# Talking-heads attention and two expert layers: the half-empty fourth key block of the V product done in 64x64 quarters

## The chip, the cores and the metric

The kernel runs on one core of one Trainium2 chip. The metric is the time of one execution on the device in microseconds (us), given as the median of several runs. All arithmetic is in 32-bit floating point.

## What is computed

The reference chains three layers. Only the first is touched by the change.

```python
# _attn_ref: batch 4, 12 heads, 448 positions, head size 64
scores = scale * np.matmul(q, k.transpose(0, 1, 3, 2))
scores = np.einsum('bhij,hg->bgij', scores, w_pre)
scores = scores - np.max(scores, axis=-1, keepdims=True)
attn = np.exp(scores)
attn = attn / (np.sum(attn, axis=-1, keepdims=True) + 1e-09)
attn = np.einsum('bhij,hg->bgij', attn, w_post)
return np.matmul(attn, v).astype(np.float32)
# reference
x = np.ascontiguousarray(attn_out.transpose(0, 2, 1, 3)).reshape(B * S, H * D)
x = _moe_ref(x=x, **moe_kwargs)        # x @ w_in, ELU, @ w_out
return _moe2_ref(x=x, **moe2_kwargs)   # x @ w_in, h * softmax(h), layer norm, @ w_out
```

The last matrix product of the attention, attn times v, is what this text calls the V product.

## The kernel before, in words

The 448 query rows of each of the four batches are cut into chunks, 17 in all (`CH`): nine of 120 columns, two each of 110, 98 and 88, one of 80 and one of 40. The chunk is the unit of the scores (L587) and of the V product (L741).

Between these two the work goes by slots of ten query rows, taken two at a time as a unit; there are 90 units. For each unit TensorE mixes the heads (`pre`, L659, into `pm`), VectorE takes the maximum (L664), ScalarE the exponential (L669, into `e`), and GpSimd scales the post-mixing weights by the reciprocal sums (L680, into `wr`). `post` (L692) multiplies the two, which mixes the heads again and turns the result over at once, so that keys lie on partitions: 28 matmuls of 64 output partitions by 60 columns into the two banks `po`. One copy per slot (L700) moves `po` to the chunk's tile `at`.

Keys are counted in blocks of 64, and 448 keys are seven of them. In `at` two blocks lie on the 128 partitions, so there are four such pairs (q = 0 to 3), and the fourth holds one block only. The kernel before fills it so: the five rows r = 0 of a slot have the seventh block on partitions 0 to 63, the five rows r = 1 have it on 64 to 127, zeros lie in the other half (`po` is cleared once at the start), and the tile of v holds the seventh block twice. The V product of a chunk is then 2 halves n of six heads, each with 24 matmuls: three pairs i of heads, four key blocks q, two heads k. The two heads of a pair go to the output partitions 0 to 63 and 64 to 127. Each half has a bank of PSUM (`sc`), which one copy (L748) empties into a tile `x`, and a DMA stores that to the scratch tensor `xs`, from which the first expert layer reads.

Each of these steps is an `op` with a rank (a planned time), the engines that may take it with a planned cost each, and the buffers that it needs. `schedule` replays the list with these costs and writes each engine's program in the order that results; six banks of PSUM are shared between the scores, `pm` and the V product. TensorE and the other engines then work through their programs strictly in that order and wait on semaphores. `AV` is the planned cost of 24 matmuls of the V product. Towards the end of the attention the first matmuls of the expert layer (L357, output `h` or `sc`) are planned in between.

## Time and profile before

| | |
|---|---|
| median of 3 runs | 1052.45 us (1050.37 to 1053.49) |
| the profiled execution, its own time | 1048.23 us |
| its span, first to last instruction | 1046.4 us |
| TensorE busy | 1017.5 us, 97% |
| VectorE, ScalarE, GpSimd busy | 742.7, 561.8, 271.2 us |
| granted TensorE clock, mean | 0.998 |

The attention takes about the first 358 us of the span; everything after it is the two expert layers. In the trace a 32-bit matmul of the attention is two instructions, so 24 matmuls of the program stand as x48. In the chain of work each piece lasts from the end of the piece before it to its own end. A matmul that gives partitions 0 to 63 and one that gives 64 to 127 can run beside each other, as can matmuls that read different halves of the 128 rows.

### The profile page before, as it was taken

What the parts mean: (1) busy time and instruction counts of PE and PEld (TensorE: products, weight loads), DVE (VectorE), ACT (ScalarE), POOL (GpSimd) and SP (SyncE); (2) the same over time, 40 slices, a digit from 0 to 9 for tenths busy, and PEclk for the clock granted to TensorE, in tenths of its full rate; (3) what the DMA queues carried; (4) which work ended last, traced back from release to release, by engine and by line L of the source; (5) the groups of instructions that cost most, each with busy time, mean ns of one, the idle gap of its engine ahead of it and who ended that gap; (6) DMA issues with size and microseconds to landing.
All of it is one profiled execution on the core that took longest, in us unless ns stands there. A gap on an engine that the chain in (4) does not pass through costs nothing.

```text
span 1046.4 us, 28479 instructions
## 1 busy us (share of the span) xinstructions
PE 1017.5 (97%) x11604; PEld 865.4 (83%) x11604; DVE 742.7 (71%) x1365; ACT 561.8 (54%) x1186; POOL 271.2 (26%) x295
## 2 busy tenths in 40 slices
PE   6799999999999999999999999999999999999998
PEld 2476776787777999889899999999999888889998
DVE  5587777678676447898979687786855355668874
ACT  3387667677778566443444344434443245555543
POOL 5011111111113324545535434434544200000000
PEclk9999999999999999999999999999999999999999
DMA  6666766876855452534523422422472533828741
GB/s 210 210 193 200 233 200 213 237 228 209 242 165 188 138 153 84 193 126 155 177 80 122 134 98 99 138 81 71 136 296 98 201 114 106 187 106 202 150 102 60
DMA packets 142442, 165.79 MB, mean 158 GB/s; under 512 B 79496, under 2 KB 119272, under 8 KB 142312
## 3 DMA queue, kind: packets, MB, share of 16 engines
q1 hardware_dynamic: 135817, 142.62, 45.7%
q0 software_dynamic: 3968, 17.30, 4.2%
q10 hardware_dynamic: 2527, 4.06, 1.2%
q8 instruction: 91, 1.49, 0.6%
q14 instruction: 39, 0.32, 0.1%
HBM read 88.02 MB, written 37.22 MB: 120 GB/s over the span
## 4 chain that ended last, share of the span: by engine, by line
PE 84%; DVE 5%; DMA 4%; issue 2%; ACT 2%; POOL 1%; ACTq 1%; POOLq 0%; DVEq 0%; SPq 0%
PE h L357 18%; PE o L898 18%; PE h L1026 11%; PE w L1098 10%; PE sc L741 7%; PE po L692 7%; PE sc L587 6%; PE pm L659 6%; DMA sp<-sev 2%; DVE x L914 1%; DVE wy L213 1%; ACTq L545 1%; PE sc L357 1%; DMA ws<-in_wi_dram 1%; ACT e L669 1%
## 5 line engine op out<-in xcount | busy, mean ns | idle before, releaser
L898 PE MATMUL o<-gh,woh 128*128 128x448 f32 x384 | 141.3, 368 | 2.8 <-DVE x L914 2.8
L898 PE MATMUL o<-glo,woh 128*128 128x448 f32 x384 | 140.0, 364 | 0.0
L898 PE MATMUL o<-gh,wol 128*128 128x448 f32 x384 | 139.6, 364 | 0.0
L669 ACT ACTIVATE e<-pm,st 128x448 f32<-128x448 f32 x180 | 115.1, 653 | 42.0 <-DVE st L664 34.3
L692 PEld LDWEIGHTS po<-wr,e 60*64 60x64 f32 x5040 | 98.6, 134 | 34.6 <-issue 18.9
L914 DVE TENSOR_TENSOR x<-x,o 128x448 f32<-128x448 f32 x168 | 102.6, 613 | 28.9 <-PE o L898 27.7
L587 PE MATMUL sc<-kt,q 64*64 64x448 f32 x816 | 106.7, 557 | 11.8 <-ACT sev L593 5.8
L664 DVE TENSOR_REDUCE st<-pm 128x1 f32<-128x448 f32 x180 | 106.0, 617 | 15.5 <-PE pm L659 14.1
L680 POOL TENSOR_TENSOR wr<-wpost_t,st 128x120 f32<-128x120 f32 x90 | 35.7, 397 | 284.5 <-DVE st L676 170.2
L692 PE MATMUL po<-wr,e 60*64 60x60 f32 x5040 | 103.0, 220 | 5.4 <-ACT at L700 2.3
L369 POOL TENSOR_TENSOR glo<-g,gh 128x448 fp32r<-128x448 f32 x64 | 78.2, 1221 | 113.4 <-ACT gh L368 110.7
L357 PE MATMUL h<-xh,wih 128*128 128x448 f32 x276 | 100.8, 365 | 0.0
L357 PE MATMUL h<-xh,wil 128*128 128x448 f32 x276 | 100.7, 365 | 0.0
L357 PE MATMUL h<-xl,wih 128*128 128x448 f32 x276 | 100.4, 364 | 0.0
L659 PE MATMUL pm<-sp,wpre_t 64*64 64x448 f32 x720 | 96.5, 545 | 3.4 <-ACT e L669 2.4
L1026 PE MATMUL h<-wi,x2h 128*128 128x512 f32 x308 | 98.8, 395 | 0.8 <-issue 0.8
L741 PEld LDWEIGHTS sc<-at,v 128*64 128x64 f32 x1632 | 76.3, 139 | 14.2 <-ACT e L669 3.5
L741 PE MATMUL sc<-at,v 128*64 128x120 f32 (+5 forms) x1632 | 83.4, 259 | 0.6 <-ACT sev L593 0.5
L898 PEld LDWEIGHTS o<-gh,woh 128*128 128x128 f32 x384 | 72.1, 188 | 11.0 <-DVE x L914 5.7
L898 PEld LDWEIGHTS o<-glo,woh 128*128 128x128 f32 x384 | 72.0, 188 | 6.1
L898 PEld LDWEIGHTS o<-gh,wol 128*128 128x128 f32 x384 | 72.1, 188 | 5.5
L587 PEld LDWEIGHTS sc<-kt,q 64*64 64x64 f32 x816 | 41.2, 136 | 40.4 <-ACT sev L593 12.2
(130 smaller groups left out, 2014.5 us busy)
## 6 DMA issues: line engine op xcount, KB each, us to landing
sp<-sev SPq DMA_DIRECT2D x90, 210.0 KB
ws<-in_wi_dram SPq DMA_DIRECT2D x33, 512.0 KB
ws<-in_wo_dram SPq DMA_DIRECT2D x21, 512.0 KB
lts<-sq SPq DMA_DIRECT2D x14, 512.0 KB
lt<-lts SPq DMA_DIRECT2D x56, 128.0 KB
q<-in_qa_dram SPq DMA_DIRECT2D x34, 192.0 KB
v<-in_vt_dram SPq DMA_DIRECT2D x24, 256.0 KB
wis<-ws POOLq DMA_DIRECT2D x12, 512.0 KB, 3.3
```

Source lines behind the costliest of these rows:

```text
L357: nc.tensor.matmul(ps[:, :S], a[:, kc * FG + ft * 128:kc * FG + (ft + 1) * 128], x[:, kc, :], start=kc == 0 and n == 0, stop=kc == ECH - 1 ...
L369: nc.gpsimd.tensor_tensor(glo, g, f(gh), ALU.subtract)
L587: nc.tensor.matmul(T[key][i][64 * x:64 * x + 64, :S], q[sl, h % 6 // 2, 64 * x:64 * x + 64], k[sl, :], start=True, stop=True)
L659: nc.tensor.matmul(ps_t[u][r][64 * s:64 * s + 64, :S], wpre_t[p, :], sp_t[c][p, g, :], start=True, stop=True)
L664: nc.vector.tensor_reduce(out=st_t[u][:P, r:r + 1], in_=ps_t[u][r][:P, :S], op=ALU.max, axis=AX.X, negate=True)
L669: nc.scalar.activation(out=t[:P], in_=ps_t[u][r][:P, :S], func=AF.Exp, bias=st[:P, r:r + 1], scale=1.0, accum_out=st[:P, 2 + r:3 + r])
L692: nc.tensor.matmul(out[:, :, 5 * r:5 * r + 5], e_t[u, r][sl, 64 * n:64 * n + 64], wr_t[u][sl, r].rearrange("p (g a) -> p g a", a=5), start ...
L741: nc.tensor.matmul(ps[64 * k:64 * k + 64, i, :], v_t[CH[c][0]][:, 6 * n + 2 * i + k, q, :], at_t[c][:, q, 6 * n + 2 * i + k, :w], start=q ...
L898: nc.tensor.matmul(ps[:, :S], a[:, ft * DM + e * 128:ft * DM + (e + 1) * 128], x, start=n == 0, stop=n == 5)
L914: nc.vector.tensor_tensor(x1[tb][:, e, :], x1[tb][:, e, :], ps[:, :S], ALU.add)
L1026: nc.tensor.matmul(ps[:, hf * 512:hf * 512 + 512], a[:, k, :], w, start=n == 0, stop=n == 3 * ECH - 1)
L1098: nc.tensor.matmul(ps[:, :384], a[:, s, k, :], w, start=k == 0 and i == 0, stop=k == 3 and i == 2)
```

## The change

The fourth key block is taken out of the 128-row matmuls and done in matmuls of 64 rows, 64 output partitions and half the columns, which is a quarter of the array each.

- `at` has a new layout: 84 lines of five rows per slot. For q below 3 a line is one (q, head, r); for q = 3 there are only the 12 heads, with r = 0 on the lower and r = 1 on the upper partitions. `post` writes `po` so, without zeros; the copy per slot is 420 elements wide and not 480, and the two clearings of `po` go.
- `whole` is what remains of the V product of a half n: 18 matmuls, with the columns ordered r = 0 first, then r = 1.
- `halves` does the fourth block: 12 matmuls. In the first group (swap 0) the lower rows, r = 0, go to the bank of n = 0 and the upper rows, r = 1, to the bank of n = 1; in the second group (swap 1) it is crossed over. So the two halves of the rows never write to one bank at the same time.
- After swap 0 half of each bank is complete: r = 0 of n = 0 and r = 1 of n = 1. Two copies take these halves out. Swap 1 is made to wait for both, and two more copies take out the other halves. The stores come behind them.
- The planned costs change: `AV` 2.6 to 1.96, `AVQ` .35 for a group of quarters, and those of the copies.
- The width of the last chunk of a batch is now the full number of slots: 90 and 100 columns in place of 88 and 98.

```diff
--- before.py
+++ after.py
@@ -503,7 +503,7 @@
 
 
     t_pre, t_post, t_av, t_sc = {}, {}, {}, {}
-    PRE, POST, AV, SC, HID = .76, .83, 2.6, .76, 3.64
+    PRE, POST, AV, AVQ, SC, HID = .76, .83, 1.96, .35, .76, 3.64
     t, nf, t_hid = T0, 0, None
 
     def plan_front():
@@ -523,7 +523,7 @@
         if pending and u - pending[0][0] == 3:
             for k in pending.pop(0)[1]:
                 t_av[k] = t
-                t += AV
+                t += AV + AVQ
         for c in range(NC):
             if last_of[c] == u:
                 pending.append((u, [(c, 0), (c, 1)]))
@@ -616,8 +616,6 @@
     def clear(t, us, r):
         return op(r, lambda e: nc.gpsimd.memset(t, 0.0), pool=us)
 
-    for t in po_p:
-        op(T0 + 2, lambda e, t=t: nc.vector.memset(t, 0.0), dve=.49)
     o_clear = {c + 3: clear(sp_t[c][:, CH[c][2]:], .38 * (NH - CH[c][2]), 4.0 + c) for c in range(2)}
 
     def begin(e):
@@ -688,17 +686,15 @@
                 for r, n, q, x in todo:
                     for s in range(ns):
                         sl = slice(64 * s, 64 * s + 60)
-                        out = ps[s][64 * x:64 * x + 64, q * 120:q * 120 + 120].rearrange("p (g a) -> p g a", a=10)
-                        nc.tensor.matmul(out[:, :, 5 * r:5 * r + 5], e_t[u, r][sl, 64 * n:64 * n + 64],
+                        out = ps[s][64 * x:64 * x + 64, :420].rearrange("p (l a) -> p l a", a=5)
+                        nc.tensor.matmul(out[:, 24 * q + r:24 * q + 24:2] if q < 3 else out[:, 72:], e_t[u, r][sl, 64 * n:64 * n + 64],
                                          wr_t[u][sl, r].rearrange("p (g a) -> p g a", a=5), start=True, stop=True)
 
         def take(e, s, u=u, sl=sl):
             c, g = sl[s]
             if c not in at_t:
-                at_t[c] = pools["at"].tile([128, 4, NH, WMAX], F32, tag="at", name="at")
-            o, n = 10 * g, min(10, width_of(c) - 10 * g)
-            copier(e)(at_t[c].rearrange("p q h r -> p (q h) r")[:, :, o:o + n],
-                      po_t[u][s][:, :480].rearrange("p (x a) -> p x a", a=10)[:, :, :n])
+                at_t[c] = pools["at"].tile([128, 84, WMAX // 2], F32, tag="at", name="at")
+            copier(e)(at_t[c][:, :, 5 * g:5 * g + 5], po_t[u][s][:, :420].rearrange("p (l a) -> p l a", a=5))
 
         r0 = t_pre[u]
         pre_op[u] = o = op(r0, pre, [o for c in {c for c, _ in sl} for o in sp_op[c]] + [o_begin, w_op], pmb, [spb_[c] for c in {c for c, _ in sl}], pe=PRE)
@@ -713,7 +709,7 @@
         o = op(r0, post, ex + [ow], pob, eb + [wb], pe=POST)
         for s, (c, g) in enumerate(sl):
             at_ops[c].append(op(r0 + 1.2 + .1 * s, lambda e, s=s, take=take: take(e, s), [o], [at_b[c]] if g == 0 else [],
-                                [pob[s]] + ([at_b[c]] if g else []), act=.45, dve=.57))
+                                [pob[s]] + ([at_b[c]] if g else []), act=.41, dve=.52))
 
 
     for c in range(NC):
@@ -729,31 +725,55 @@
 
             for i in range(6):
                 ov.append(op(t_av[c, 0] - VD + 4 * i if b else T0 + 8 + 2.5 * i, lambda e, i=i, load=load: load(e, i), [o_begin], [] if i else [vb], [vb] if i else [], sp=.5, lag=4.0))
+        G = CH[c][2]
+        av_of, x_of = [Buf("sc", range(6 if c else 3)) for _ in range(2)], [Buf("x") for _ in range(2)]
+
+        def whole(e, n, c=c, G=G, av_of=av_of):
+            x_t[c, n] = av_of[n].tile()[:, :30 * G].rearrange("p (k w) -> p k w", k=3)
+            for i in range(3):
+                for q in range(3):
+                    for k in range(2):
+                        h = 6 * n + 2 * i + k
+                        nc.tensor.matmul(x_t[c, n][64 * k:64 * k + 64, i, :], v_t[CH[c][0]][:, h, q, :], at_t[c][:, 24 * q + 2 * h:24 * q + 2 * h + 2, :5 * G],
+                                         start=i == 0 and q == 0, stop=False, skip_group_check=True)
+
+        def halves(e, swap, c=c, G=G):
+            for i in range(3):
+                for r in range(2):
+                    n, p = (r + swap) % 2, slice(64 * r, 64 * r + 64)
+                    for k in range(2):
+                        h = 6 * n + 2 * i + k
+                        m = nc.tensor.matmul(x_t[c, n][64 * k:64 * k + 64, i, 5 * G * r:5 * G * r + 5 * G], v_t[CH[c][0]][p, h, 3, :], at_t[c][p, 72 + h, :5 * G],
+                                             start=False, stop=swap == 1, skip_group_check=True)
+                        if swap and i == 0:
+                            for x in T["half", c]:
+                                tc.add_manual_dep(m.ins, x.ins.name, mybir.DependencyInfo(mybir.DependencyClass.Sync, mybir.DependencyReason.DATA), reason="halves")
+
+        def second(e, whole=whole, halves=halves):
+            whole(e, 1)
+            halves(e, 0)
+
+        part = 10 * G / 120
+        o = op(t_av[c, 0], lambda e, whole=whole: whole(e, 0), at_ops[c] + ov, av_of[:1], [vb, at_b[c]], pe=AV * part)
+        o = op(t_av[c, 1], second, [o], av_of[1:], [vb, at_b[c]] + av_of[:1], pe=AV * part + AVQ)
+
+        def take(e, n, r, c=c, G=G):
+            if r == n:
+                T["x", c, n] = pools["xt"].tile([128, 3, WMAX], F32, tag="x", name="x")
+            T.setdefault(("half", c), []).append(copier(e)(T["x", c, n][:, :, :10 * G].rearrange("p k (g r a) -> p k g r a", r=2, a=5)[:, :, :, r],
+                                                           x_t[c, n][:, :, 5 * G * r:5 * G * r + 5 * G].rearrange("p k (g a) -> p k g a", a=5)))
+
+        def store(e, n, c=c, w=w):
+            b, r, _ = CH[c]
+            dst = xs[b][n * 384:n * 384 + 384, r:r + w]
+            dma(dst.rearrange("(k p) w -> p k w", k=3), T["x", c, n][:, :, :w])
+
+        r0 = t_av[c, 1] + AV
+        first_half = [op(r0 + .4 + .1 * n, lambda e, n=n, take=take: take(e, n, n), [o], [x_of[n]], [av_of[n]], act=.28, dve=.26) for n in range(2)]
+        o = op(r0 + .9, lambda e, halves=halves: halves(e, 1), first_half, [], [vb, at_b[c]] + av_of, pe=AVQ)
         for n in range(2):
-            r = t_av[c, n]
-            xb, avb = Buf("x"), Buf("sc", range(6 if c else 3))
-
-            def mm(e, c=c, n=n, w=w, avb=avb):
-                ps = x_t[c, n] = avb.tile()[:, :3 * w].rearrange("p (k w) -> p k w", k=3)
-                for i in range(3):
-                    for q in range(4):
-                        for k in range(2):
-                            nc.tensor.matmul(ps[64 * k:64 * k + 64, i, :], v_t[CH[c][0]][:, 6 * n + 2 * i + k, q, :], at_t[c][:, q, 6 * n + 2 * i + k, :w],
-                                             start=q == 0, stop=q == 3)
-
-            o = op(r, mm, at_ops[c] + ov, [avb], [vb, at_b[c]], pe=AV * w / 120)
-
-            def take(e, c=c, n=n, w=w):
-                T["x", c, n] = pools["xt"].tile([128, 3, WMAX], F32, tag="x", name="x")
-                copier(e)(T["x", c, n][:, :, :w], x_t[c, n])
-
-            def store(e, c=c, n=n, w=w):
-                b, r, _ = CH[c]
-                dst = xs[b][n * 384:n * 384 + 384, r:r + w]
-                dma(dst.rearrange("(k p) w -> p k w", k=3), T["x", c, n][:, :, :w])
-
-            o = op(r + AV + .2, take, [o], [xb], [avb], act=.36, dve=.42)
-            T["xs", c, n] = op(r + AV + 1, store, [o], [], [xb], sp=.5, more=.2)
+            o2 = op(r0 + .9 + .6 + .1 * n, lambda e, n=n, take=take: take(e, n, 1 - n), [o], [], [av_of[n], x_of[n]], act=.28, dve=.26)
+            T["xs", c, n] = op(r0 + .9 + 1.5, lambda e, n=n, store=store: store(e, n), [o2, first_half[n]], [], [x_of[n]], sp=.5, more=.2)
 
 
     last = None
```

On TensorE, around the second half of chunk 2 (120 columns; `sc<-kt,q` are scores, `pm` is `pre`, `po` is `post`, `sc<-at,v` the V product), the order before is:

```order
L692 MATMUL po_109<-wr,e 64x12x5
L587 MATMUL sc<-kt,q 64x448 x4
L741 MATMUL sc<-at,v 64x120 x24
L587 MATMUL sc<-kt,q 64x448 x4
L659 MATMUL pm<-sp,wpre_t 64x448 x4
L587 MATMUL sc<-kt,q 64x448 x4
L692 MATMUL po_108<-wr,e 64x12x5
```

And at the same place after the change:

```order
L690 MATMUL po_109<-wr,e 64x60
L587 MATMUL sc<-kt,q 64x448 x4
L737 MATMUL sc<-at,v 64x120 x18
L746 MATMUL sc<-at,v 64x60 x12
L587 MATMUL sc<-kt,q 64x448 x4
L657 MATMUL pm<-sp,wpre_t 64x448 x4
L746 MATMUL sc<-at,v 64x60 x12
L690 MATMUL po_108<-wr,e 64x12x5
```

The 24 matmuls have become 18 with the first group of quarters right behind them; four score and four `pre` matmuls then stand between the two groups.

On ScalarE the copies of chunk 2 stand so before (`sev<-sc` takes scores out, `e` is the exponential, `at<-po` the copy per slot):

```order
L748 COPY x<-sc 128x360
L700 COPY at<-po_108 128x48x10
L593 COPY sev<-sc 128x448
L748 COPY x<-sc 128x360
L593 COPY sev<-sc 128x448
L669 ACTIVATE e,st<-pm,st 128x448
```

And so after, where one of the two early copies is on ScalarE (the other is on VectorE) and both late ones are on ScalarE:

```order
L763 COPY x<-sc 128x36x5
L593 COPY sev<-sc 128x448 x2
L803 ACTIVATE kst<-kst 128x192
L763 COPY x<-sc 128x36x5 x2
L667 ACTIVATE e,st<-pm,st 128x448 x2
```

Two copies of 360 elements per chunk have become four of 180.

On TensorE at the last chunk, among the first matmuls of the expert layer (`sc<-xh,wih` and the like, 128 rows), the order before is:

```order
L357 MATMUL sc<-xl_6350,wih 128x448
L357 MATMUL sc<-xh_6349,wil 128x448
L741 MATMUL sc<-at,v 64x98 x48
L357 MATMUL sc<-xh_6349,wih 128x448
L357 MATMUL sc<-xl_6350,wih 128x448
```

After the change, with 30 matmuls of the expert layer between the two groups of quarters:

```order
L737 MATMUL sc<-at,v 64x100 x36
L746 MATMUL sc<-at,v 64x50 x12
L357 MATMUL sc<-xh_6598,wih 128x448
L357 MATMUL sc<-xl_6599,wih 128x448
...
L357 MATMUL sc<-xh_6598,wil 128x448
L746 MATMUL sc<-at,v 64x50 x12
L357 MATMUL h<-xT_6859,wih 128x448 x2
```

The second group has moved away from the first, into the run of 128-row matmuls.

## Rows read from the trace of the kernel before

**Rows 1.** The page, part 1: busy time, share of span, instructions.

```profile
PE 1017.5 (97%) x11604; PEld 865.4 (83%) x11604; DVE 742.7 (71%) x1365; ACT 561.8 (54%) x1186; POOL 271.2 (26%) x295
```

**Rows 2.** Busy time by stretch of the span: length, engines (instructions), clock, DMA share, GB/s.

```profile
core 0: us, PE busy (x) PEld busy (x) DVE busy (x) ACT busy (x) POOL busy (x), PEclk, DMA share, GB/s
...
180.00:240.00 60.00, 59.34 (x1558) 46.30 (x1554) 44.91 (x116) 44.37 (x119) 6.81 (x18) 1.00 0.78 230
...
300.00:336.00 36.00, 33.90 (x950) 26.65 (x952) 25.96 (x67) 26.43 (x71) 8.78 (x14) 1.00 0.57 175
336.00:357.00 21.00, 20.97 (x500) 18.87 (x492) 8.20 (x16) 11.67 (x23) 8.95 (x8) 1.00 0.53 161
357.00:400.00 43.00, 43.00 (x216) 39.83 (x213) 22.57 (x30) 28.85 (x53) 12.72 (x10) 1.00 0.44 133
```

**Rows 3.** Chain that ended last, 60 to 345 us: shares; start, length, what.

```profile
by line: PE sc L741 25.6%; PE po L692 24.8%; PE sc L587 20.3%; PE pm L659 20.2%; issue 3.0%; ACT e L669 2.2%; DVE st L664 1.3%; ACT at L700 0.7%; ACT sev L593 0.5%; PE sc L357 0.3%; POOL wr L680 0.3%; POOL xl L248 0.3%; DVE at L700 0.2%; DV
...
67.59 1.81 PE sc L741 x48
...
142.00 2.41 PE sc L741 x48
...
202.91 2.17 PE sc L741 x48
```

**Rows 4.** The same chain, in the stretch around one chunk of 120 columns.

```profile
162.42 2.61 PE sc L741 x48
165.03 0.97 PE po L692 x56
166.00 0.76 PE pm L659 x8
...
167.51 0.81 PE po L692 x56
168.32 0.76 PE sc L587 x8
169.08 2.61 PE sc L741 x48
171.69 0.91 PE sc L587 x8
```

**Rows 5.** The same chain at the last chunk (both halves, 98 columns).

```profile
352.94 4.19 PE sc L741 x96
```

**Rows 6.** The same chain near the attention's start.

```profile
46.62 8.07 DMA sp<-sev
```

**Rows 7.** Groups by shape, 60 to 345 us: count, busy us, mean ns, idle before.

```profile
L700 ACT COPY at<-po 128x480 f32<-128x480 f32 x87 | 50.0, 590 | 12.9 <-PE po L692 12.8
L700 DVE COPY at<-po 128x480 f32<-128x480 f32 x76 | 49.3, 652 | 26.7 <-PE po L692 26.1
...
L593 DVE COPY sev<-sc 128x448 f32<-128x448 f32 x69 | 41.5, 617 | 14.2 <-PE sc L587 12.0 <-DMA sp<-sev 0.9 <-PE po L692 0.6
...
L748 ACT COPY x<-sc 128x360 f32<-128x360 f32 x17 | 7.8, 459 | 16.4 <-PE sc L741 16.2
...
L700 ACT COPY at<-po 128x384 f32<-128x384 f32 x3 | 1.5, 512 | 0.0
...
L748 DVE COPY x<-sc 128x360 f32<-128x360 f32 x1 | 0.5, 533 | 2.2 <-PE sc L741 2.2
```

**Rows 8.** Line L748 (34 copies): its engines' idle time, total and times.

```profile
  PE sc L741: 29.4, 25
```

**Rows 9.** ScalarE in order of time; in brackets, idle time before and releaser.

```profile
171.74 0.46 ACT L748 COPY x<-sc 128x360 f32<-128x360 f32 x1 [1.48 <-PE sc L741]
```

**Rows 10.** The chain again, where the last units of the attention run out.

```profile
332.00 0.86 issue
332.86 0.40 POOL wr L680
333.26 0.74 POOL xl L248
```

## The prediction

> **What bounds the kernel now.** I read the page's busy shares first: TensorE is busy for 97% of the span, VectorE 71%, ScalarE 54% [rows 1]. That is a mean over stages, so the table by stretch comes next [rows 2]. In the middle of the attention TensorE is busy 59.34 of 60 us at a granted clock of 1.00, VectorE and ScalarE about 45 of 60. Only where the units run out (300 to 336 us) does TensorE fall to 33.9 of 36. The chain of waits says the same [rows 3]: from 60 to 345 us 25.6 + 24.8 + 20.3 + 20.2 + 0.3 = 91% of it is TensorE, and the V product alone is 25.6% of 285 us, 73 us. About 9%, 25 us, goes through the other engines or through waits without a name. Before 54.7 us the chain lies on a transfer of scores [rows 6], so chunk 0, whose V product stands there, counts for nothing. From 336 us on, and into the expert layers, TensorE has no gap (20.97 of 21 and 43.00 of 43 us), so a microsecond taken from TensorE between 60 and 357 us should be a microsecond of the total.
>
> **The price of a V matmul.** A half of 24 matmuls takes 1.81 us at 80 columns, 2.17 at 98, 2.41 at 110 [rows 3] and 2.61 at 120 [rows 4]. That is a straight line of 0.020 us per column with 0.21 us over. Two heads go side by side, so the 48 instructions are 24 pairs, each costing 0.83 ns per column. Part of the 0.21 us is the change of shape: two halves in a row at 98 columns take 4.19 us [rows 5] and not 2 x 2.17 = 4.34, so coming to the 128-row shape costs 0.15 us. The other 0.06 us is 2.5 ns per pair. Going back costs as much: `post` takes 0.97 us behind a V product and 0.81 behind scores, scores 0.91 against 0.76 [rows 4], hence 0.16 us.
>
> **Removed.** Per half 6 of 24 matmuls, so per chunk 12 instruction pairs. At 120 columns a pair is 100 + 2.5 = 102.5 ns, which makes 1.23 us per chunk. By the same line 110 columns give 1.13; the chunks of 98 and 88, which also grow by two columns, give 0.95 and 0.85; the one of 80 gives 0.83. The sum is 9 x 1.23 + 2 x (1.13 + 0.95 + 0.85) + 0.83 = 17.8 us.
>
> **Added.** 24 matmuls per chunk that fill a quarter of the array each. The trace has their like: the 56 instructions of `post`, 64 output partitions by 60 columns, in four quarters with the two row halves in different banks, take 0.81 us when no change of shape precedes them [rows 4]. That is 14 rounds of four at 57.9 ns. The change needs 48 instructions, 12 rounds, per chunk: 0.695 us at 120 columns, where a quarter has the same 60 columns. In narrower chunks a round lies between 57.9 ns (if something other than the columns sets it) and 7.9 ns plus 0.83 ns per column. Summed over 16 chunks that is 11.1 or 10.3 us, a balance of -6.6 or -7.4. No row tells which, so I take the middle, -7.0. Changes of shape stay as many, since the first group takes over the one that the next operation had paid, with two exceptions in the new order. Chunk 1 has both its 128-row parts in a row (-0.31). At the last chunk the second group stands alone among 128-row matmuls of the expert layer, which I price as three more changes (+0.47, an estimate from the 0.15 and 0.16 above). Balance on TensorE: **-6.8 us**.
>
> The weak point is whether the quarters run four at a time. In the V product two matmuls that use the same 128 rows and different output halves already overlap: a pair takes 102.5 ns where one alone would stream for 100 [rows 4]. In `post` all four overlap. The Trainium skill, "TensorE: Matmul & The Clock Gate", section "Part 3: Packing small matmuls — row/col tiling", says that a weight load overlaps with running matmuls only when the row group differs. By that rule the two heads of a V product would follow each other, which this trace contradicts (2.61 us for a half, not at least 4.8). The new groups issue two quarters on the lower rows and then two on the upper, where `post` alternates, so the rule stays a rival below.
>
> **Copies.** The copy per slot shrinks by 60 elements. ScalarE's price is (590 - 512) / 96 = 0.81 ns per element, VectorE's (652 - 617) / 32 = 1.09 [rows 7]; over 180 copies that is some 10 us less. The 34 copies of `x` (0.46 us at 360 elements on ScalarE, 0.53 on VectorE) become 68 of 180 elements, by the same prices 0.31 and 0.34 us each: some 6 us more. Both engines have a quarter of their time free [rows 2], so I count nothing. The finer scatter, runs of five in place of ten, is not in the trace. Runs of ten cost VectorE no more per element than a plain copy, so I take nothing. If each run of five cost as much as ten, 180 copies would be longer by 0.4 us, 72 us over two engines, which would use up half of their free time and start to hold TensorE up. The two cleared banks go from a stretch that waits for transfers.
>
> **The new wait.** The second group waits for two copies, and everything on TensorE is queued behind it. What hides the copies is the work between the groups: in six chunks four score and four `pre` matmuls or their like, 0.76 + 0.75 = 1.5 us; in one `post` and `pre`, in one only a `post` (0.81 to 0.97); otherwise more. The copies need 0.05 us to start when their engine is already waiting (a V product ended at 169.08 + 2.61 = 171.69, its copy began at 171.74 [rows 4, 9]) and 0.31 us, or 0.65 if both are on one engine: 0.4 to 0.7 us. In 25 of 34 cases the copying engine sat waiting for the V product [rows 8]. When it is one operation late (some 0.6 us) the cover still holds; two late, TensorE stands. I put 0.5 us on all chunks together; without any cover it would be 16 x 0.55, about 9 us. The banks of the V product are also held longer, from the first 18 matmuls to the last copies, some 9 us for the first bank (2.0 + 1.7 between + 2.3 + 1.5 + 0.4 + 0.7) where it was 2.6 + 0.05 + 0.46 = 3.1, which leaves scores and `pre` fewer of six: 0.5 us, a choice, between nothing and the 25 us now off TensorE.
>
> **Where gains are lost.** A saving inside the 9% of the chain that other engines set is not kept: 0.6 us. At the end GpSimd delays weights for `post` by a long subtraction [rows 10]. The new order puts the last two `post` together, with no expert matmuls between them, but also sets fewer long subtractions before the last weights. I leave these two at nothing, with 2 us either way in the range.
>
> **Sum.** -6.8 + 0.5 + 0.5 + 0.6 = -5.2 us. Against the profiled execution's own time, 1048.23, that is 1043.0. That execution was 4.2 us below the median of the runs shown, and the forecast is for the median: 1052.45 - 5.2 = **1047.2 us**.
>
> **Rivals.**
> - *Stalls eat it.* TensorE waits at the second groups, or for banks, 0.2 to 0.4 us more per chunk, 3 to 6 us in all; from 0.4 on nothing is left. For it speaks that nine of 34 copies found their engine busy; against it the covers of 1.5 us. Time about 1051 to 1053.
> - *Quarters on the same rows follow each other.* 24 rounds per chunk instead of 12: 22.2 us added for 17.8 removed, and with 0.2 and 1.6 from above +6.2, so 1058.7. It decides from a round of (17.8 - 1.8) / 192 = 83 ns. The overlap in [rows 4] speaks against it. This is the case that ends slower.
> - *More than the matmuls.* The program is re-planned and the copy engines get lighter: the whole 6.8 and about 3 of the 25 us off TensorE go, 1042.6.
> - *Fine scatter is charged.* Slower by several us, as worked out above.
>
> **How the numbers follow.** Forecast 0.60 (own range 1045 to 1049.2), stalls 0.18, quarters in series 0.07, more than the matmuls 0.12, scatter 0.03. The runs before spread over 3 us, so 0.3%, 3.2 us, is about what can be told from no change. Faster (below 1049.3) is the forecast and the third rival: 0.72; same 0.18; slower 0.10. The range leaves out the slower cases and the far end of the third: 1043.0 to 1052.5.
>
> **What would show it.** Right: pieces of 36 instructions at 120 columns of about 0.15 + 18 x 0.1025 = 2.0 us, groups of 24 quarters at 0.35 us (0.16 more behind a 128-row part), the next operation back at 0.76 or 0.81, copies of `x` near 0.31 us, copies of `at` near 0.54 (ScalarE) and 0.59 (VectorE). Wrong: groups of 0.7 us, waits of TensorE for a copy of `x`, a larger share of the chain on ScalarE or VectorE, or a stand before the last two `post`.

## The result: slower by 1.0%

The changed kernel takes 1063.38 us (median of 10 runs, 1059.0 to 1068.69) where the kernel before takes 1052.17 (10 runs, 1048.59 to 1057.29). The ratio is 1.0101, with a 95% interval of 1.0073 to 1.0129, which makes +10.6 us; the forecast was -5.2. Medians, ratios and clocks below leave out one execution of e13 that fell into a slower state of the chip (1059.76 us). The profiled execution of after took 1059.0 us, with a span of 1057.1, against [rows 1 to 10] from one of 1048.23.

**What the sum had right.** The chain of waits of after (start us, length, what) shows the pieces in the sizes of the prediction:

```profile
173.43 0.34 PE sc L746 x24
...
192.14 2.00 PE sc L737 x36
194.14 0.51 PE sc L746 x24
...
196.15 0.33 PE sc L746 x21
196.48 2.73 issue
199.21 0.27 PE sc L746 x2
...
295.77 0.33 PE sc L746 x24
...
349.24 0.59 ACT at L697
...
351.19 1.01 issue
352.20 0.39 PE po L690 x4
352.58 0.51 ACT at L697
...
353.23 1.13 PE po L690 x56
354.36 2.18 PE sc L357 x6
356.54 3.52 PE sc L737 x59
```

A 128-row part at 120 columns (L737) takes 2.00 us where a half took 2.61 [rows 4]; a group of quarters (L746) takes 0.34, or 0.51 behind a 128-row part. Quarters do run four at a time. In the narrower chunks, for which the prediction had taken the middle between two prices, a group of 24 with 40 or 45 columns still takes 0.33 us (295.77 above, 45 columns): a round of four hardly gets shorter with its columns, so the dearer of the two prices held (11.1 us in all, not 10.3). By the reading of the Trainium skill that the prediction weighed ("TensorE: Matmul & The Clock Gate", section "Part 3: Packing small matmuls — row/col tiling"), that weights load behind running matmuls only in another row group, pairs on the same rows would follow each other and a group would take about twice as long; the 0.34 us says that they don't. The copies also came out as costed: groups by shape, 60 to 345 us (count, busy us, mean ns, idle before):

```profile
L697 ACT COPY at<-po 128x420 f32<-128x420 f32 x82 | 45.6, 574 | 16.4 <-PE po L690 16.2
L697 DVE COPY at<-po 128x420 f32<-128x420 f32 x78 | 45.5, 591 | 18.2 <-PE po L690 14.9 <-ACT e L667 1.9 <-ACT kst L803 1.1
...
L763 ACT COPY x<-sc 128x180 f32<-128x180 f32 x20 | 5.9, 330 | 15.2 <-PE sc L746 15.2
L763 DVE COPY x<-sc 128x180 f32<-128x180 f32 x12 | 4.0, 343 | 8.8 <-PE sc L746 7.2 <-DMA sp<-sev 1.5
```

The finer scatter costs ScalarE little (574 ns for an estimated 540), VectorE nothing (591 for 590), and the half copies of `x` 330 and 343 ns (310 and 340).

**Where the time went.** Busy shares hide it (TensorE 96% after, 97% before). Two views of after show it: busy time by stretch (columns as in [rows 2]), and what TensorE waited for from 45 to 370 us (total us, times, longest).

```profile
55.80:58.30 2.50, 0.02 (x3) 0.00 (x0) 1.29 (x4) 0.94 (x3) 0.00 (x0) 0.90 0.10 34
58.30:61.70 3.40, 3.34 (x58) 3.34 (x59) 0.36 (x1) 0.28 (x2) 0.00 (x0) 0.58 0.66 193
...
180.00:240.00 60.00, 55.05 (x1540) 41.85 (x1532) 42.45 (x115) 41.36 (x114) 6.59 (x17) 1.00 0.75 212
...
336.00:357.00 21.00, 16.25 (x488) 13.50 (x486) 14.01 (x29) 14.82 (x34) 12.95 (x12) 0.95 0.55 151
354.70:358.10 3.40, 3.40 (x26) 2.73 (x26) 2.34 (x3) 2.47 (x4) 1.66 (x1) 0.51 0.91 253
```

```profile
PE po L690 <- issue: 6.0, 9, 1.0
PE sc L746 <- issue: 4.8, 4, 2.7
PE sc L737 <- ACT at L697: 2.5, 1, 2.5
PE pm L657 <- issue: 2.3, 1, 2.3
PE po L690 <- POOL wr L678: 1.9, 2, 1.3
```

From 180 to 240 us TensorE is busy 55.05 us where it was 59.34, and from 336 to 357 us 16.25 where it was 20.97 [rows 2]. In the second stretch before has matmuls of the expert layer between the last `post`, which after does behind them. The waits are mostly "issue", time that no semaphore explains, in the middle of runs of one line: 2.73 us inside one group of quarters. No wait for a copy of `x` (L763) stands among TensorE's waits, so the wait that the change adds did no harm by itself. At 55.8 us chunk 1's first part waits 2.5 us for a copy of `at`, and for the next 3.4 us TensorE works at a granted clock of 0.58, near the lower of its two levels (1.2 GHz); the same happens at 354.7, behind the last two `post`.

I split the time to the first output matmul of the expert layer (line `o`) by the records of the trace. Idle: no matmul runs. Clock: half of TensorE's busy time at half clock. Work: the rest. After that point all four executions take 680.0 to 680.9 us.

```
                first o at   idle  clock   work
before             365.7     21.2    1.7   342.8
before again       371.2     25.2    4.4   341.7
after              376.3     32.7    6.3   337.3
after again        381.3     36.6    6.8   337.9
```

On the mean of two executions work fell by 4.7 us (forecast 6.8), idle time rose by 11.5 and the clock took 3.5 more.

**The stalls named "issue".** The records of the DMA queue "instruction" are transfers of 16 KB: 48 of them in the kernel before and 49 after, from 60 to 300 us. I counted TensorE's instructions (a weight load and a matmul each): 256 lie between transfers, one block. The long "issue" stalls end at one position of a block, instruction 193 or 194 modulo 256, 1.3 to 1.8 us behind the landing of a transfer. So these are waits for TensorE's own program. Within 0.6 us of that position, from 45 us to the first `o`, stood 3.6 and 5.2 us of stalls in the two executions of before, 15.4 and 12.8 in the two of after. This sum is called the stalls at the block edges below.

### The profile page after: what moved, and what is told of

Read it like the earlier page. It is cut to its first block, busy times and chain, and to the rows that moved or that the text cites. A ratio compares the mean times of both kernels' runs of the same rounds, so it can differ in the third digit from the quotient of the medians.

```text
span 1057.1 us, 29349 instructions
## 1 busy us (share of the span) xinstructions
PE 1016.5 (96%) x12012; PEld 861.4 (81%) x12012; DVE 742.1 (70%) x1392; ACT 556.8 (53%) x1191; POOL 272.3 (26%) x295
## 4 chain that ended last, share of the span: by engine, by line
PE 81%; DVE 5%; issue 3%; DMA 2%; ACT 1%; POOL 1%; SPq 0%; POOLq 0%; DVEq 0%; ACTq 0%
PE h L357 18%; PE o L918 17%; PE h L1046 11%; PE w L1118 10%; PE po L690 7%; PE pm L657 6%; PE sc L737 6%; PE sc L587 5%; PE sc L746 1%; DVE x L934 1%; DVE wy L213 1%; PE sc L357 1%; DMA ws<-in_wi_dram 1%; DMA wis<-ws 1%; POOL ws L260 1%
## 5 line engine op out<-in xcount | busy, mean ns | idle before, releaser
L587 PE MATMUL sc<-kt,q 64*64 64x448 f32 x816 | 110.0, 564 | 9.2 <-ACT sev L593 4.3
L209 DVE SCALAR_TENSOR_TENSOR wq<-ws,wq 128x512 int32<-128x512 int32 (+1 forms) x70 | 70.9, 1013 | 1.1
L737 PEld LDWEIGHTS sc<-at,v 128*64 128x64 f32 x1224 | 59.2, 141 | 14.5 <-issue 4.5
L737 PE MATMUL sc<-at,v 128*64 128x120 f32 (+5 forms) x1224 | 66.2, 264 | 4.4 <-ACT at L697 2.5
```

The lines of the kernel that those rows point to most:

```text
L587: nc.tensor.matmul(T[key][i][64 * x:64 * x + 64, :S], q[sl, h % 6 // 2, 64 * x:64 * x + 64], k[sl, :], start=True, stop=True)
L737: nc.tensor.matmul(x_t[c, n][64 * k:64 * k + 64, i, :], v_t[CH[c][0]][:, h, q, :], at_t[c][:, 24 * q + 2 * h:24 * q + 2 * h + 2, :5 * G], ...
```

## Experiments

The first pair runs both kernels once more; its stretches are the "again" rows above.

> The kernel before once more, for a second profile. Supply theory: waits at the block edges near the first profile's 2.8 us. It also shows whether the start (first post of unit 6 at 62.5 us, 67.9 in the changed kernel) is a matter of the order or differs from run to run: within 1 us of 62.5 if it is the order.

> The changed kernel once more, for a second profile. Supply theory: 10 to 20 us at the block edges, not always at the same edges, since what delays a block is the traffic on its transfer queue. The start within 1 us of 67.9 if it is the order.

One run each, 1053.04 and 1064.01 us. The stalls at the block edges are again more after than before (12.8 against 5.2 us). The first `post` of unit 6 starts at 64.2 us, 1.7 later than in the first execution of before and so outside the 1 us expected, and at 67.6 in after (67.9): after starts later in both, but a third of that gap can differ between executions of one order.

**Is it the supply of instructions?** Four kernels add instructions or take them away.

```diff
 e1_split, in the V product of before
+for z in ([slice(0, w // 2), slice(w // 2, w)] if q % 2 else [slice(0, w)]):
 e2_after_post128 and e3_before_post128, in post
-for r, n, q, x in todo:
+for r, q, x in [(0, 3, 0), (1, 3, 1)] + [(r, q, None) for r in range(2) for q in range(3)]:
+    p = slice(0, 128) if x is None else slice(64 * x, 64 * x + 64)
 e11_before_posts2, the list of post of before twice
+... for q in range(3)] * 2 + [[(0, 6, 3, 0), (1, 6, 3, 1)]] * 2:
```

> The kernel before, in its own order, but in the V product the matmuls of the key blocks q = 1 and 3 are cut into two of half the columns: same columns streamed, no new wait, copy, bank or order, 1632 more TensorE instructions in the trace (23451 to 25083; the change added 837). Supply theory (TensorE's program comes in blocks of 256 instructions, one block ahead, and a dense run of instructions reaches the block's edge before it has come): waits without a named releaser inside runs of one line, 256 or a multiple of it apart in TensorE's instruction count, 10 us or more of them, and 8 to 25 us slower than before. Wait theory (the new waits for copies and the banks held longer cost the time) and plan theory (the re-planned order is worse): only 408 more pairs at 2.5 ns, 1 us slower, at most 2.

1067.89 us, ratio 1.0148 (1.008 to 1.0216): +15.6 us. A half of 120 columns took 2.78 where it took 2.61, but one of 80 columns took 2.36 to 2.58 where it took 1.81, and in the trace the V product as a whole takes 91.0 us of TensorE's work where it took 80.2 and 80.5 in the two executions of before. So some 10.7 of the 15.6 us are TensorE's own pace, and what is left lies within the interval. What speaks for the supply here is the trace alone: 12.1 us of stalls at the block edges.

> The changed kernel, in its own order, with post writing two key blocks per matmul (128 output partitions in place of twice 64) for q below 3: 16 matmuls in place of 28, the same 14 rounds of 60 columns, 4320 fewer TensorE instructions (24288 to 19968). Supply theory: the waits without a releaser (about 13 us between 60 and 362 us in the changed kernel) fall below 3 us. If the new shape is free, 10 to 14 us faster than the changed kernel, about 1050. A change between 64 and 128 output partitions may cost as much as that between 64 and 128 rows, 0.15 us; with two to three of them for each of 90 posts it would take up to 30 us, and then the total rises while the waits still fall. Wait and plan theories: the waits stay as they are, within 3 us.

> The kernel before with the same wider post. It prices the shape alone: before has some 3 us of waits without a releaser, so supply theory gives -3 us plus the price of the shape, which must be the same as in e2. The difference e2 minus e3 is then the change without hindrance from the supply: about -5 us by the supply theory, still about +10 by the two others.

1109.93 and 1109.17 us, ratios 1.0577 (1.0509 to 1.0646) and 1.0546 (1.0497 to 1.0594). `post` with 128 output partitions takes 1.60 us (104.32 in the chain of e2) instead of 0.81, so TensorE is the bound again; "issue" falls to 0.0% and 0.4% of their chains. But the change shows no gain here either (by the ratios +3.3 us, with intervals too wide to exclude either of the differences expected): up to the first `o` of the two traces work falls by 8.8 us, and clock (+6.8) and idle time (+2.2) take it back.

> The kernel before with every post issued twice, the second time over the same banks with the same numbers: some 10,000 more instructions for TensorE (90 times 112), nothing else added. The price of the supply by itself. A post takes 0.81 us, so by TensorE's own pace the time grows by 90 x 0.81 = 73 us, to 1125 (no limit of supply: 1115 to 1135, hardly any stall at the block edges). Supply theory: 256 instructions (one block) can't be had in less than some 4.0 us (blocks with less work than that took 3.9 to 4.0 us on the average in all traces so far) and often need 5; some 100 blocks lie between the first posts and the expert layer with 3.6 us of work each, so the attention takes 400 to 500 us in place of 300, the total 1150 to 1250, with stalls at the edges of most blocks.

1174.95 us, ratio 1.1166 (1.1119 to 1.1213): +122 us, inside the range of the supply theory. `post` takes 161.9 us of TensorE's work where it took 78.6 and 79.2, so 83 of the 122 are its own pace (73 were expected), and the stalls at the block edges are 42.9 us. The chain's shares of e11 from 60 to 430 us:

```profile
by line: PE po L692 37.1%; PE sc L741 18.7%; PE pm L659 17.7%; PE sc L587 15.9%; issue 9.2%; DMA xs<-x 0.8%; DVE at L700 0.3%; ACT x L748 0.1%; ACT sev L593 0.1%; ACT e L669 0.1%; DVE st L676 0.0%; DVE st L664 0.0%; DVEq L700 0.0%; DVEq L66
```

Nothing but instructions was added, and "issue" goes to 9.2% (3.0% before [rows 3]). Blocks with less than 4.0 us of work (71 of the 98 from 62 us to the first `o`) took 4.07 us on the average here, and 3.9 to 4.1 in the traces of before, after, e1, e4 to e10. So supply is a limit in dense stretches: shown. That it is the whole loss of the change is not, as the next ones show.

**Is it the order?** Numbers of the plan alone are changed.

```diff
 e4_after_late: the second group and its copies
-r0 + .9
+r0 + 3.4
 e8_after_tail (e9_before_tail: + 6, in the kernel before)
-t0 = t_pre[first[lc]]
+t0 = t_pre[first[lc]] - 6
 e10_after_spaced
-t += AV + AVQ
+t += 2.6
 e12_after_both: e8's edit, and (which moves the first two copies as well)
-r0 = t_av[c, 1] + AV
+r0 = t_av[c, 1] + AV + 2.5
 e15_after_plan: e8's edit, and
-t += AV + AVQ
+t += AV + (1.5 if k[0] < 2 else AVQ)
```

> The changed kernel with the second group of quarters planned 2.5 us later, so that more work stands between the groups (a post and mostly eight more matmuls in nearly all chunks); the rest of the order is planned anew. Wait theory: the stands at the second group go, 1047 to 1052. Supply theory: no fewer instructions, so 10 us or more of waits without a releaser remain, 1056 to 1066. Plan theory: anything, by a changed order; the unnamed waits tell.

1060.28 us, ratio 1.0087 (1.0051 to 1.0123): by the ratios 1.5 us less than after, which is within the intervals. At the block edges stand 10.7 us of stalls, as the supply theory expected.

> The changed kernel with one number of the plan changed: the time from which the first weights and activations of the expert layer are prepared is set 6 us earlier, so that 6 and 12 matmuls of the expert layer stand ahead of the last two post again, as before the change. The start and the middle of the attention keep the order of the changed kernel. Order theory (about 8 us of the loss come from the end of the attention, where nothing stands between the last posts): from post 80 to the first output matmul of the expert layer 43 to 47 us where the changed kernel has 51 to 52, and a total of 1055 to 1058.5. Rival, supply alone (TensorE's instructions arrive too slowly wherever post and quarters lie close together, and what stands between the last posts does not matter): total 1062 to 1065, the stretch 50 us or more.

1057.75 us, ratio 1.0061 (1.0034 to 1.0088), by the ratios 4.2 us less than after, with intervals that still touch: the total that the order theory expected, but not its place, so this is no proof of it. From post 80 to `o` its trace still has 49.8 us (51.1 in after, 43.2 in before).

> The kernel before, with one number of the plan changed: the same preparation set 6 us later, so that the last three post lie together and all matmuls of the expert layer come behind them, as in the changed kernel. No quarters, no new copies. Order theory: the stretch from post 80 to the first output matmul grows from 43 to 47 to 52 us, total 1056 to 1061. Rival, supply alone: the number of TensorE's instructions is that of before, so the total stays at 1050 to 1054.

1053.94 us, ratio 1.0019 (0.9994 to 1.0044), as the rival expected: the order of the tail alone hardly slows the kernel before.

> The changed kernel, planned with the distances of before: a half of the V product takes 2.6 us in the plan's times (it took 2.31), so that all planned times are those of before; costs and instructions are those of the change. The first 18 matmuls of a chunk and its next 18 are apart again at the start, and 18 matmuls of the expert layer stand between the last posts. Order theory: start back to 63 to 65 us, end to 43 to 48, the middle as in the changed kernel (257 to 260 us), total 1050 to 1056. Supply theory: block-edge stalls stay at 12 to 16 us, total 1059 to 1064.

1062.92 us, ratio 1.0078 (1.0046 to 1.011), as the supply theory expected; at the block edges 11.2 us of stalls, a little less than it expected. The first `post` of unit 6 is back at 63.7 us, so the order at the start was restored and gained nothing that can be told from noise.

> The changed kernel with two numbers of the plan: the preparation of the expert layer 6 us earlier (so that 6 matmuls of it stand behind each of three of the last posts) and the second group of quarters with its copies 2.5 us later. If what the two gave apart (5.7 and 3.2 us) adds up: 1053 to 1056, as fast as before. Supply theory: the blocks of TensorE's program are as dense as in the changed kernel except at the end, so that most of the loss of the middle stays: 1055 to 1060.

1064.23 us, ratio 1.0107 (1.0068 to 1.0147). Neither expectation holds: nothing of what e8 had gained is left, although the stalls at the block edges are down to 6.6 us in this trace. Half clock takes 12.3 us in it (6.3 in after).

> The changed kernel, whole, with two numbers of its plan: after each half of the first two chunks 3.46 us are planned in place of 2.31, so that chunk 1's two 128-row parts are apart again with a post and scores between them, and the preparation of the expert layer is 6 us earlier, so that matmuls of the expert layer stand behind each of the last posts. If the order at start and end is what the rest of the change costs (7.6 us in e13 against e14): 1063.4 - 7.6 = 1056, or less (1053 to 1057.5), at a granted clock of 0.993 or more. If it is the finer copies, the copies of x in two parts and the waits: 1060 to 1064.

1058.95 us, ratio 1.0083 (1.0055 to 1.0112), between the two expectations. In every order the changed kernel is slower than before, by 0.6 to 1.1%, and no kernel that does the whole computation beat the kernel before.

**Which part of the change costs what?** These leave out quarters.

```diff
 e5_third (a third of the quarters), e13_after_none (none)
-for i in range(3):
+for i in range(1):      # e13: range(0)
 e14_before_none, in the V product of before
-for q in range(4):
+for q in range(3):
 e16_none_plan: e13 with the plan of e15
 e17_none_onecopy: e13, copies of x in one part
-T["x", c, n][:, :, :10 * G]...[:, :, :, r], x_t[c, n][:, :, 5 * G * r:5 * G * r + 5 * G]...
+T["x", c, n][:, :, :10 * G]..., x_t[c, n][:, :, :10 * G].rearrange("p k (r g a) -> p k g r a", r=2, a=5)
 e18_before_twocopies: e14, each copy of x in two ops
+h = slice(0, w // 2) if part == 0 else slice(w // 2, w)
```

> The changed kernel in its own order, with only the first of the three pairs of heads in each group of quarters (4 of 12 matmuls; it leaves out two thirds of the fourth key block). Waits, copies, banks and order stay; TensorE has 1088 fewer instructions (24288 to 23200, 251 below the kernel before) and 17 x 12 x 2/3 rounds at 57.9 ns less work, 7 to 8 us. Supply theory: the waits at the edges of the 256 blocks go from 15.9 us back to 5 or less, so that 15 us or more are saved: 1044 to 1049. If the groups cost only their own rounds, or the cost lies in waits for copies, banks or the order: 1055 to 1057, and the waits stay.

1053.37 us, ratio 1.0008 (0.9979 to 1.0037), between the two expectations: 10 us less than after, of which 7.1 are the 128 rounds left out. TensorE has fewer instructions than before, yet the stalls at the block edges stay, 12.6 us in its trace. So the number of instructions alone does not set them: the supply theory fails here in that form.

> The changed kernel without any group of quarters: it leaves out the fourth key block of the V product. The order of the changed kernel, the finer scatter of the copies, the copies of x in two parts and the new waits all stay. Against the kernel before, TensorE loses the 17.8 us of the removed matmuls and about 800 instructions. Supply theory (what hurt are the 96 instructions per chunk that the quarters add where TensorE's program is dense): 1034 to 1040, within 3 us of e14_before_none. Rival, the rest of the change (new order at start and end, copies, waits): 1043 to 1049, at least 6 us above e14_before_none.

1048.45 us, ratio 0.9969 (0.9935 to 1.0003), 6.7 us above e14 (6.4 by the ratios), as the rival expected. One part of the expectation does not hold: the new wait is put on matmuls of the second group of quarters, and with none left it is gone from e13, and from e16 and e17 as well.

> The kernel before without its matmuls on the fourth key block (18 per half in place of 24): it leaves that block out. Plan, order and copies are those of before; TensorE has the same matmuls as in e13_after_none. If a microsecond taken from TensorE is a microsecond of the total, 1052.4 - 17.8 = 1034.6 (1032 to 1037). If the supply of instructions already holds the kernel before at some 51 to 53 per us, only the roughly 800 instructions less count, some 15 us, and stalls at the block edges grow: 1036 to 1041.

1041.76 us, ratio 0.9908 (0.9874 to 0.9941). This is the run that settles most. 17.8 us of matmuls are simply gone, nothing is added or moved, and 9.7 us come back, less than either expectation. Its chain from 60 to 320 us:

```profile
by line: PE po L692 18.6%; PE sc L587 15.7%; PE pm L659 15.2%; PE sc L741 14.6%; DMA sp<-sev 12.6%; DMA q<-in_qa_dram 4.5%; DMA xs<-x 4.2%; ACT e L669 3.4%; issue 2.9%; DVE st L664 2.6%; ACT at L700 1.9%; ACT sev L593 1.0%; SPq L545 1.0%; D
366 pieces in order of time: start us, us, what
...
93.01 5.73 DMA q<-in_qa_dram
211.81 5.14 DMA sp<-sev
226.27 6.02 DMA sp<-sev
256.44 9.78 DMA sp<-sev x2
269.04 5.86 DMA q<-in_qa_dram
```

and TensorE's waits for transfers in it, from 45 to 370 us (total us, times, longest):

```profile
PE sc L587 <- DMA q<-in_qa_dram: 6.1, 3, 3.1
...
PE pm L659 <- DMA xs<-x: 1.8, 1, 1.8
...
PE pm L659 <- DMA sp<-sev: 1.2, 2, 0.6
```

In before 91% of the chain was TensorE, and no transfer is among the lines named [rows 3]; here TensorE has 64% and transfers 21%, and TensorE itself stands 9.1 us for transfers. How large the share is differs from execution to execution. The chains from 60 to 320 us of the second execution of before (e6) and of e18, which has the matmuls of e14 and below takes the same time, are:

```profile
by line: PE sc L741 24.1%; PE po L692 23.4%; PE sc L587 20.1%; PE pm L659 18.0%; DMA sp<-sev 4.1%; issue 2.6%; DMA q<-in_qa_dram 2.0%; ACT at L700 1.4%; ACT e L669 1.3%; DVE st L664 0.8%; ACT sev L593 0.6%; DVE sev L593 0.6%; DVE at L700 0.
by line: PE po L692 22.9%; PE sc L587 20.5%; PE pm L659 17.4%; PE sc L741 17.0%; issue 4.7%; ACT e L669 3.6%; DMA sp<-sev 2.8%; DMA q<-in_qa_dram 2.1%; DVE st L664 1.9%; DMA kst<-in_wo_dram 1.8%; ACT at L700 1.6%; DVE at L700 1.0%; ACT sev 
```

So transfers stood in the chain of before already, with 6% in e6, and in e18 they share what is not TensorE's (78%) with "issue": 7% and 5%. The same stretch of 240 us by busy time, of before:

```profile
60.00:300.00 240.00, 236.46 (x6136) 175.00 (x6128) 181.06 (x467) 178.04 (x476) 27.25 (x70) 1.00 0.72 216
```

and of e14:

```profile
60.00:300.00 240.00, 230.46 (x5972) 164.51 (x5972) 183.76 (x475) 180.90 (x484) 27.93 (x72) 0.99 0.73 220
```

The 16 DMA engines are busy 72% and 73% of it, and move 216 and 220 GB/s: TensorE has less to do, and the transfers bring its inputs hardly faster. The engines are not full, so what holds the transfers back is not shown. One rival was not run, a kernel whose order is planned for the shorter halves: e14 keeps the order of before, and another might give back more.

> e13_after_none (no quarters, which leaves out the fourth key block) with the same two numbers of the plan. It has the copies and waits of the change, and about the order of before. If order costs the 7.6 us: down to the 1041.8 of e14_before_none, 1040 to 1044. If copies and waits do: 1047 to 1051.

1049.16 us, ratio 0.9988 (0.996 to 1.0015): about the order of before at start and end doesn't bring it down to e14.

> e13_after_none (no quarters, which leaves out the fourth key block) with the copies of x of a chunk in one part again, one per half, as before the change; the order of the columns, the finer scatter of the copies of at and the planned times stay those of the change. If the split of the copies of x and what waits for it cost the 7.5 us that e13 and e16 stand above e14: 1040 to 1044. If the finer scatter and the columns in another order do: 1047 to 1051.

1045.08 us, ratio 0.9944 (0.9907 to 0.998), between the two expectations.

> e14_before_none (before, without the fourth key block) with each copy of x cut in two halves of its columns, the second half planned 0.7 us later; everything else as in e14. If the split costs the 7.5 us: 1047 to 1051. If the finer scatter does: 1040 to 1044, as e14.

1042.0 us, ratio 0.9895 (0.986 to 0.993), as e14: splitting the copies of `x` costs nothing by itself, which the prediction had. e17 lies between e13 and e14, and its interval reaches both.

**The clock and the edges: what the 6.4 us between e14 and e13 go with.** The mean granted clock over the runs of a kernel goes with the order at the start. Where both 128-row parts of chunk 1 stand in a row, it is 0.9904 (after), 0.9902 (e2), 0.992 (e5), 0.9908 (e8), 0.9908 (e12), 0.9901 (e13), 0.9907 (e17) and 0.993 (e4). Where they stand apart, it is 0.9951 (before), 0.9935 (e1), 0.9955 (e3), 0.9943 (e9), 0.9937 (e10), 0.9947 (e14), 0.9964 (e15), 0.9948 (e16) and 0.9945 (e18); only e11, with its doubled `post`, has 0.9895. Between e13 and e14 the clock differs by 0.0046, which is 4.8 us of 1050, most of the 6.4. But e15 and e16 have the clock back, and by the ratios e15 gained 1.9 us from after and e16 lost 2.0 from e13, both within the intervals. So the clock alone does not explain the 6.4 us.

The record has a second candidate. The stalls at the block edges are 6.0 us in e14 and 8.4 in e18, but 11.7, 13.5 and 12.2 in e13, e16 and e17, which have as few instructions. TensorE's longest waits from 45 to 370 us (total us, times, longest) are in e13

```profile
PE po L690 <- issue: 7.8, 4, 4.8
```

and in e16

```profile
PE po L690 <- issue: 13.0, 7, 4.3
```

e14 has 1.7 us at the same place and e18 5.4. These are single executions, and nothing here says why the new order or the new copies should leave the program later at its block edges: the cause of the 6.4 us stays open.

## Why the prediction was wrong

By ratios the +10.6 us come apart in three, since e14 and e13 have the same matmuls on TensorE (and neither has the new wait):

```
                                           forecast   measured
matmuls removed      (before to e14)        -17.8       -9.7  (-13.2 to -6.2)
order, copies        (e14 to e13)            +0.8       +6.4  (about +-5)
quarters, their wait (e13 to after)         +11.8      +13.9  (about +-5)
sum                                          -5.2      +10.6
```

The last forecast is 10.8 for the quarters, 0.5 for the changes of shape at the last chunk and 0.5 for the new wait; the middle one is 0.5 for banks and 0.6 for gains lost, less 0.3 for chunk 1. The wide intervals are those of ratios 0.0061 and 0.0132 apart, each known to some 0.003.

- *"From 336 us on, and into the expert layers, TensorE has no gap ..., so a microsecond taken from TensorE between 60 and 357 us should be a microsecond of the total."* This step failed, and costs 8.1 of the 15.8 us. With the matmuls left out, 9.7 of 17.8 us came back (e14), and transfers had 21% of the chain where none was named before. A chain that is 91% TensorE says what ended last in one execution, not how far behind the next bound is, and another execution of the same kernel had 86%, with 6% on transfers (e6). [Rows 2] had a hint in a column that I did not use, a DMA share of 0.78 between 180 and 240 us; that this share sets the bound is argued, not shown. "Where gains are lost: 0.6 us" counted only the 9% that other engines already had.
- *"Both engines have a quarter of their time free, so I count nothing"* and *"I leave these two at nothing"*, the order. The sum had 0.8 us for all that is not matmuls or their wait, and 6.4 were measured. The prices of the copies held, and cutting the copies of `x` in two costs nothing in the order of before (e18). "The program is re-planned" stood only in a rival, as a gain. The new order put chunk 1's parts in a row at the start, where one waits 2.5 us and half clock follows, and the last two `post` together; the sum had no term for the clock. But with the parts apart and the clock back e16 is no faster than e13, so what of the 6.4 us is order and what is copies stays open.
- *The price of the quarters* (0.34 and 0.16 us) was right to 0.01 us at 120 columns; in the narrow chunks the dearer of the two prices held, 0.4 us more than the middle. The rest of the 2.1 us over the forecast lies within the interval. A cause may be that the quarters add 96 instructions per chunk for the 48 removed, where TensorE's program stalls at block edges (15.4 and 12.8 us in after, 11.7 in e13): argued, not shown.
- *The rivals*: "stalls eat it" had the direction but the wrong place (copies, banks), "quarters in series" and "fine scatter" fell. What would show it wrong was named: a stand before the last two `post` is there (0.59, 0.51 us for copies at 349.24 and 352.58 in the chain, and 1.01 at a block edge at 351.19), yet by e9 the order of the tail costs +2.0 us (-0.6 to +4.6) in the kernel before.

Open stay how much of the 6.4 us is copies (e17 against e13 and e14 can't tell), and why TensorE's program comes late at some block edges and not at others. That its transfers wait behind those of the data would fit the DMA share, but I found no dependence on the traffic of the stretch around them.

## What to carry to other kernels

A chain that is nearly all one engine prices a saving only up to the next bound: take a second execution to see what else stands in the chain, and first run a kernel that just leaves the matmuls out (e14), which shows what a cheaper way of doing them can bring at most in that order. Count instructions as well as time where TensorE's pieces are small, since a half-empty matmul replaced by twice as many small ones saves time and may cost supply. And in a planned kernel compare the new order at the places where an engine comes out of a wait, because a stand there was followed by half clock here.

## What the hardware showed that I had not expected

- TensorE's program comes in 16 KB transfers of 256 instructions, on the DMA engines that also carry data. From 60 to 300 us TensorE took 2 x 6136 / 240 = 51.1 instructions per us before, and 52.4 (2 x 6285) after with stalls; in e11, with a DMA share of 0.55 from 200 to 380 us, 2 x 5418 / 180 = 60.2. Blocks with less than 4.0 us of work took 3.9 to 4.1 on the average.
- The same `post` with 60 rows and 128 output partitions takes 1.60 us where two matmuls of 64 output partitions take its place in 0.81.
- Behind a wait of 2.5 us (granted clock 0.90) came 3.4 us of full work at 0.58. In before, where TensorE was busy 6.80 of the 7 us from 55 to 62, the clock was 1.00.
